# Causal mask of four head pairs: from a product on TensorE to a select on GpSimd, with the staircase loaded as seven rows

## The chip, the cores and the metric

The kernel runs on one core of one Trainium2 chip. The metric is the device time in microseconds (us) from launch to end; lower is better. Engines are called by the profile's short names: PE (TensorE, matmuls), PEld (its weight loads), DVE (VectorE), ACT (ScalarE), POOL (GpSimd) and SP (SyncE, which here only issues DMAs).

## The reference

Two stages. First causal attention with a selective decay, over 8 batches x 8 heads, 576 tokens, head size 64:

```
scores = q @ k.T / 8
cum    = cumsum(max(s, 0))
bias   = min(-(cum[query] - cum[key]), 0)
scores = where(key > query, -1e9, scores + bias)
attn   = softmax(scores) @ v
```

Then a feed-forward block on the 4608 tokens x 512: `h = x @ w_in` (512 to 2048), `g = h * clip(h + 3, 0, 6) / 6`, `out = g @ w_out` (2048 to 512). The output is float32; the kernel multiplies in float16.

## The kernel before

**Pairs and slots.** The 64 heads are taken as 32 pairs, p = 0 to 31; pairs p*4 to p*4+3 belong to one batch (`PPB` = 4). The main loop over p is called a slot here. In slot p PE computes the scores of pair p for both heads (hh = 0, 1), the second head's attention-times-V of pair p-1, the first head's of pair p, and transposes the q and k of pair p+1. From slot 4 on (`p == PPB` has code of its own) matmuls of the feed-forward are strung between these pieces by `group()`: a call takes the next entry of `plan`, "1" for one `m1` (four 128x512 matmuls into a PSUM tile `ph`; then a Relu on ACT into `tr`, L562, and a min-times on DVE into `gT`, L563) or "2" for one `m2` (four into `po`), "." for none. The order on each engine is the program's order; nothing reorders it.

**Scores.** Per head there are three groups, each filling one PSUM bank `S` and followed by one exp on ACT (L422) into the tile `P`. Group 0 has the four diagonal 128x128 blocks (L388), groups 1 and 2 the blocks below the diagonal (L403). The last 64 tokens of both heads are the `corner` (`Sc`, L454; exp into `PC`, L462). From slot 4 on the `S` and `Sc` tiles rotate over two banks, so a group can start only when the exp of the group two before it is done.

**Causal mask of the diagonal blocks, two ways.** For p < `NPROD` = 8 a matmul of 2 x identity with the constant `shut` (minus 65504 above the diagonal) opens the bank: L377, 512 columns, once per head, and L441, 128 columns, once per corner. For p >= 8 this matmul isn't there. Instead rows 68 to 127 of the `qk` tile hold a staircase of 60 steps, so that the scores' own matmul (128 rows instead of 68) pushes most of the masked part far down, and after the exp `shut_out` on POOL (L426, affine_select) sets what lies above the diagonal to zero: `pool_mid` for head 0's group 0, `pool_end` for the corner and head 1's group 0. Their readers are the diagonal blocks of `av(p, hh, 1)` (L481).

**Staircase.** `stair_sb` is loaded once in slot 2; `set_stair` copies it into rows 64 to 127 of a `qk` slot (there are four, pair p uses p % 4): on POOL in slots 5 to 7 (L695, one copy per head), on ACT in slots 8 and 9. Rows 64 to 67 are then overwritten by `load_aug`, two small DMAs that bring the decay's rows.

**Tokens out of order.** Pairs 3 to 6 (`mixed`) have their queries in another order, for which there is a second constant, `shutm`.

**POOL and SP.** In slots 4 to 7 POOL runs, in this order: the loads `tok` of pair p+3 (DMAs issued by POOL), weight chunks (`load_w_in` = `I`, `load_w_out` = `U`), then `pool_mid`: `cast_v(p+1)` (two casts, L206 and L207, which wait for the V of pair p+1) and `set_stair`; then `load_aug`. POOL waits there for no exp. SP issues the loads of V, `load_v(p+2)`, three DMAs each.

Of the kernel before, what the change touches and what calls it, by code (L numbers as in the profile page):

```python
# [10 lines left out]
F16 = mybir.dt.float16  # L11
# [3 lines left out]
NEG_BIG = -1200.0  # L15
# [3 lines left out]
def kernel(  # L19
# [30 lines left out]
    NVRAW = 2  # L50
    VW = 66
    NROW = 1
    NWARM = (11, 2, 6)
    HALVES = (slice(0, 288), slice(288, SEQ))

    grp = (np.arange(128) * 61 // 128)[None, :]
    steps_r = np.arange(1, 61)[:, None]  # L60
    stair = np.zeros((128, 2, 128), np.float32)
    stair[68:, 0] = np.where(grp < steps_r, 1.0, 0.0)
    stair[68:, 1] = np.where(grp == steps_r, NEG_BIG, 0.0)
    stair_dram = nc.inline_tensor(stair.astype(np.float16), name="stair")
# [30 lines left out]
    stair_sb = keep("stair_sb", [128, 2, 128], F16)  # L95
# [63 lines left out]
    def load_aug(p, eng):  # L159
        for hh in range(2):  # L160
            g = 2 * p + hh
            eng.dma_start(  # L162
                out=qks[p % NQK][64:68, hh, :, 64 * hh : 64 * hh + SEQ],
                in_=rows_of[g // 32].rearrange("(r g) i t -> g r i t", g=32)[
                    g % 32, :, slice(0, 3, 2) if mixed(p, 0) else slice(1, 3), 0:SEQ
                ],
            )

    def load_w_in(c):
        nc.gpsimd.dma_start(  # L170
# [102 lines left out]
    def mixed(p, i):  # L273
        return i == 0 and PPB - 1 <= p < NPROD - 1
# [82 lines left out]
    def Pof(p, hh):  # L357
        return Ps[(2 * p + hh) % 3]
# [10 lines left out]
    def scores(p, hh, g):  # L369
        qT, kT = qk_of(p, hh)  # L370
        pt = Pof(p, hh)
        S = s_bank([128, 512], "S")
        by_product = p < NPROD
        if g == 0:
            rows = slice(0, 68 if by_product else 128)
            if by_product:
                mm(  # L377
                    S.rearrange("p (t c) -> p t c", c=128),
                    lhsT=ident2,
                    rhs=(shutm if mixed(p, 0) else shut)[:, None, :].to_broadcast(  # L380
                        [128, 4, 128]
                    ),
                    start=True,
                    stop=False,
                )
            for j in range(4):
                c = slice(128 * j, 128 * (j + 1))
                mm(  # L388
                    S[:, c],
                    lhsT=kT[rows, c],  # L390
                    rhs=qT[rows, c],
                    start=(j == 0 and not by_product),
                    stop=(j == 3 and p >= NROW),
                )
            if p < NROW:
                for j in range(4):
                    c = slice(128 * j, 128 * (j + 1))
                    by_rows(p, hh, S[:, c], c, c, j == 3)
        else:
            for j in ((0, 3) if g == 1 else (1, 2)):  # L400
                c = OFF[j] - 512 * g
                w = 448 - 128 * j
                mm(  # L403
                    S[:, c : c + w],
                    lhsT=kT[0:68, 128 * j : 128 * (j + 1)],
                    rhs=qT[0:68, 128 * (j + 1) : SEQ],
                    start=(c == 0),
                    stop=(c != 0 and p >= NROW),
                )
# [12 lines left out]
        nc.scalar.activation(out=pt[:, c], in_=S, func=AF.Exp, scale=0.125)  # L422

    def shut_out(ap, w):
        part = ap.rearrange("p (t c) -> p t c", c=w)
        nc.gpsimd.affine_select(  # L426
            out=part,
            in_=part,
            pattern=[[0, part.shape[1]], [1, w]],
            compare_op=ALU.is_ge,  # L430
            fill=0.0,
            base=0,
            channel_multiplier=-1,
        )

    def corner(p):
        S = s_bank([128, 2, 64], "Sc")
        by_product = p < NPROD
        rows = slice(0, 68 if by_product else 128)
        if by_product:  # L440
            mm(  # L441
                S,
                lhsT=ident2,
                rhs=(shutm if mixed(p, 0) else shut)[:, None, 0:64].to_broadcast(
                    [128, 2, 64]
                ),
                start=True,
                stop=False,
            )
        for hh in range(2):  # L450
            qT, kT = qk_of(p, hh)
            if p < NROW:
                by_rows(p, hh, S[:, hh, :], slice(512, 640), slice(512, 576))
            mm(  # L454
                S[:, hh, :],
                lhsT=kT[rows, 512:640],
                rhs=qT[rows, 512:576],
                start=(hh == 0 and not by_product),
                stop=(hh == 1),
            )  # L460
# [232 lines left out]
    def set_stair(i, copy, heads=(0, 1)):  # L693
        for hh in heads:
            copy(  # L695
                out=qks[i][64:128, hh, :, 64 * hh : 64 * hh + 640].rearrange(
                    "p i (t c) -> p i t c", c=128
                ),
                in_=stair_sb[64:128, :, None, :].to_broadcast([64, 2, 5, 128]),
            )  # L700

    fill(nc.vector, xT[:, 0, 0:SEQ], 0.0)

    def warm(n):
# [125 lines left out]
    load_aug(1, nc.gpsimd)  # L830
    load_v(1, nc.sync)
    load_aug(2, nc.sync)
    cast_v(0)
    for i in range(2):
        load_qk(3, i)
# [11 lines left out]
    for p in range(NP):  # L847
# [25 lines left out]
                crossbar_qk(p + 2)  # L873

        def pool_mid():
            if p >= NPROD:
                shut_out(Pof(p, 0)[:, 0:512], 128)
            if nxt:
                cast_v(p + 1)
            if p in (5, 6, 7):  # L880
                set_stair((p + 3) % NQK, nc.gpsimd.tensor_copy)
            if p == 13:
                new_rest()
                cum4(1, nc.gpsimd, whole)
                cum5(1, nc.gpsimd.tensor_copy, whole)

        def pool_end():
            if p >= NPROD:
                shut_out(PCs[p % 2][:, 0:128], 64)
                shut_out(Pof(p, 1)[:, 0:512], 128)  # L890
            if p >= NPROD and p != 9 and p + 2 < NP:
                if p == 14:
                    cum6(1, nc.gpsimd, whole)
                load_aug(p + 2, nc.gpsimd)

        if p >= PPB:
            for fn, c in {
                4: ((I, 2),),
                5: ((I, 3),),
                6: ((U, 0), (U, 1), (U, 2), (U, 3)),  # L900
                7: ((U, 4), (U, 5), (U, 6), (U, 7)),
            }.get(p, ()):
                fn(c)
        if PPB <= p < NPROD:
            pool_mid()
            if p == 4:
                load_aug(7, nc.gpsimd)
            elif p in (6, 7):
                load_aug(p + 2, nc.gpsimd)

        if p and p + 2 < NP:
# [40 lines left out]
        if p == PPB:  # L952
            early[0] = False
            scores(p, 0, 0)
            av(p - 1, 1, 0)
            av(p - 1, 1, 1)
            norm(p - 1, 1)
            m1_begin(0, 0, NKC - 1)
            scores(p, 0, 1)
            transpose_x(p - 1)  # L960
            m1_begin(0, 1, NKC - 1)
            pt = transpose_in(p + 1, 0)
            transpose_out(p + 1, 0, pt, pars=(0,))
            group()
            transpose_out(p + 1, 0, pt, pars=(1,))
            scores(p, 0, 2)
            group()
        else:
            scores(p, 0, 0)
            if p >= NPROD:  # L970
                pool_mid()
# [11 lines left out]
        if p == 12:  # L983
            cum2(whole)
        corner(p)
        if p in (8, 9):
            set_stair(3, nc.scalar.copy, (p - 8,))
        elif p == 11:
            new_sum()
            cum1(1, whole)  # L990
        group()
# [3 lines left out]
            get(1)  # L995
            av(p, 0, 0)
        scores(p, 1, 0)
        if p >= NPROD:
            pool_end()
        if PPB < p < NPE - 1:  # L1000
            get(1)
        elif p == 3 * PPB:
# [62 lines left out]
```

## Time and profile before

| | us |
|---|---|
| median of 3 runs (354.74 to 355.49) | 354.82 |
| the profiled execution, whole | 354.79 |
| its span in the profile | 353.1 |
| PE busy in the span | 345.1 (98%) |
| DVE, ACT, POOL busy | 230.2, 224.7, 169.7 |
| L377 matmuls | 16 of 128x512 |
| L441 matmuls | 8 of 128x128 |
| L695 staircase copies | 6 on POOL, 2 on ACT, 1.25 each |

The granted PE clock is full all through. Slots by PE's order in the trace: slot 4 from 25.55 to 34.17, slot 5 to 41.26, slot 6 to 48.39, slot 7 to 57.26, slot 8 to 64.40, slot 9 to 73.64. The profiler's time for one matmul (379 ns for 128x512) overlaps with the next one's; the spacing of starts is what a matmul costs in a row of them.

### The profile page before, as it was taken

What the parts mean: (1) busy time and instruction counts of PE and PEld (TensorE: products, weight loads), DVE (VectorE), ACT (ScalarE), POOL (GpSimd) and SP (SyncE); (2) the same over time, 40 slices, a digit from 0 to 9 for tenths busy, and PEclk for the clock granted to TensorE, in tenths of its full rate; (3) what the DMA queues carried; (4) which work ended last, traced back from release to release, by engine and by line L of the source; (5) the groups of instructions that cost most, each with busy time, mean ns of one, the idle gap of its engine ahead of it and who ended that gap; (6) DMA issues with size and microseconds to landing.
All of it is one profiled execution on the core that took longest, in us unless ns stands there. A gap on an engine that the chain in (4) does not pass through costs nothing.

```text
span 353.1 us, 7778 instructions
## 1 busy us (share of the span) xinstructions
PE 345.1 (98%) x2926; PEld 191.0 (54%) x2926; DVE 230.2 (65%) x476; ACT 224.7 (64%) x397; POOL 169.7 (48%) x296
## 2 busy tenths in 40 slices
PE   8999999999999999999999999999999999999995
PEld 3775666555555555555555555555555444444442
DVE  7996997676868677666666666757654544544531
ACT  6987896787787667666776666666664334443310
POOL 8977799676778656455555555555310000000000
PEclk9999999999999999999999999999999999999999
DMA  9999999999999999998798959997120100101112
GB/s 164 152 208 209 199 185 182 117 181 196 154 136 100 190 219 188 173 211 186 168 167 198 179 144 197 181 180 164 38 75 14 59 29 34 59 2 59 59 50 72
DMA packets 144782, 48.35 MB, mean 137 GB/s; under 512 B 130648, under 2 KB 139784, under 8 KB 144744
## 3 DMA queue, kind: packets, MB, share of 16 engines
q1 hardware_dynamic: 117112, 37.54, 54.0%
q0 software_dynamic: 27392, 10.03, 24.8%
q8 instruction: 23, 0.38, 0.4%
q10 hardware_dynamic: 240, 0.28, 0.2%
q14 instruction: 15, 0.12, 0.1%
HBM read 37.36 MB, written 9.44 MB: 133 GB/s over the span
## 4 chain that ended last, share of the span: by engine, by line
PE 90%; DVE 4%; ACT 3%; issue 1%; DMA 1%; ACTq 0%
PE po L574 35%; PE ph L547 34%; PE O L481 7%; PE S L403 7%; PE S L388 4%; DVE qk L310 1%; PE pt L266 1%; ACT P L422 1%; DMA s_all<-in_s_dram 1%; DVE x L504 1%; PE ptx L518 1%; PE Sc L454 1%; ACT tr L562 1%; PE S L377 1%; DVE qk L332 1%
## 5 line engine op out<-in xcount | busy, mean ns | idle before, releaser
L563 DVE SCALAR_TENSOR_TENSOR gT<-tr,ph 128x512 f16<-128x512 f32 x144 | 98.9, 687 | 97.6 <-ACT tr L562 96.5
L547 PE MATMUL ph<-xT,w_in_sb 128*128 128x512 f16 x576 | 148.1, 379 | 0.0
L574 PE MATMUL po<-w_out_sb,gT 128*128 128x512 f16 x576 | 145.9, 379 | 0.0
L562 ACT ACTIVATE tr<-ph,bias 128x512 f32<-128x512 f32 x144 | 99.0, 688 | 73.0 <-PE ph L547 70.6
L422 ACT ACTIVATE P<-S 128x512 f16<-128x512 f32 x192 | 111.3, 595 | 37.5 <-PE S L388 22.3
L547 PEld LDWEIGHTS <-w_in_sb 128*128 128x128 f16 x576 | 51.4, 97 | 44.2
L574 PEld LDWEIGHTS <-gT 128*128 128x128 f16 x576 | 50.0, 97 | 46.5 <-issue 0.2
L426 POOL TENSOR_SCALAR_AFFINE_SELECT P<-P 128x512 f16<-128x512 f16 x48 | 31.3, 651 | 44.4 <-ACT P L422 44.4
L403 PE MATMUL S<-qk 68*128 68x448 f16 (+3 forms) x256 | 49.0, 272 | 0.5 <-ACT P L422 0.5
L481 PE MATMUL O<-va,P 128*128 128x65 f16 x896 | 47.9, 193 | 0.3 <-ACT P L422 0.3
L481 PEld LDWEIGHTS <-P 128*128 128x128 f16 x896 | 39.2, 97 | 14.0 <-ACT P L422 0.5
L230 DVE COPY qk<-jt 64x768 f16<-64x768 f16 x84 | 36.8, 439 | 1.2
L403 PEld LDWEIGHTS <-qk 68*128 68x128 f16 x256 | 23.7, 98 | 24.5 <-issue 0.9
L162 POOL DMA_DIRECT2D qk<-rows_of x56 | 32.8, 588 | 1.1 <-PE S L403 0.3
L504 DVE TENSOR_TENSOR x<-O,rl 128x320 f16<-128x320 f32 x64 | 31.5, 492 | 2.2
L590 DVE TENSOR_SCALAR ob<-po 128x512 f32<-128x512 f32 (+1 forms) x36 | 24.3, 676 | 8.3 <-PE po L574 7.6
L388 PEld LDWEIGHTS <-qk 128*128 128x128 f16 (+1 forms) x256 | 18.9, 97 | 14.0 <-DVE qk L310 1.7
L426 POOL TENSOR_SCALAR_AFFINE_SELECT PC<-PC 128x128 f16<-128x128 f16 x24 | 7.0, 293 | 39.9 <-ACT PC L462 39.8
L388 PE MATMUL S<-qk 128*128 128x128 f16 (+1 forms) x256 | 24.8, 219 | 1.0 <-DVE qk L332 0.5
L206 POOL CAST va<-vraw 128x512 f16<-128x512 f32 x32 | 21.0, 656 | 4.7 <-DMA vraw<-in_v_dram 2.4
L310 DVE COPY qk<-pt 64x576 f16<-64x576 f16 x22 | 17.6, 805 | 6.2 <-ACT qk L310 5.9
L202 POOL CAST tok<-raw 128x576 f16<-128x576 f32 x28 | 18.0, 679 | 0.0
(79 smaller groups left out, 201.9 us busy)
## 6 DMA issues: line engine op xcount, KB each, us to landing
out_dram<-ob SPq DMA_DIRECT2D x35, 256.0 KB, 2.0
vraw<-in_v_dram SPq DMA_DIRECT2D x64, 128.0 KB, 4.0
raw<-in_q_dram SPq DMA_DIRECT2D x14, 288.0 KB
raw<-in_k_dram SPq DMA_DIRECT2D x14, 288.0 KB
tok<-in_q_dram POOLq DMA_DIRECT2D x18, 144.0 KB, 5.2
tok<-in_k_dram POOLq DMA_DIRECT2D x18, 144.0 KB, 5.9
w_in_sb<-in_moe_w_in_dram POOLq DMA_DIRECT2D x4, 512.0 KB, 8.5
w_out_sb<-in_moe_w_out_dram POOLq DMA_DIRECT2D x8, 256.0 KB, 7.1
```

The lines of the kernel that those rows point to most:

```text
L162: eng.dma_start(out=qks[p % NQK][64:68, hh, :, 64 * hh : 64 * hh + SEQ], in_=rows_of[g // 32].rearrange("(r g) i t -> g r i t", g=32)[g % ...
L230: copies[par](out=qk[0:64, :, i, 128 * par : 128 * par + 256 * n].rearrange("p h (s two c) -> p h s two c", two=2, c=128)[:, :, :, 0, :], ...
L388: mm(S[:, c], lhsT=kT[rows, c], rhs=qT[rows, c], start=(j == 0 and not by_product), stop=(j == 3 and p >= NROW),)
L403: mm(S[:, c : c + w], lhsT=kT[0:68, 128 * j : 128 * (j + 1)], rhs=qT[0:68, 128 * (j + 1) : SEQ], start=(c == 0), stop=(c != 0 and p >= NROW),)
L422: nc.scalar.activation(out=pt[:, c], in_=S, func=AF.Exp, scale=0.125)
L426: nc.gpsimd.affine_select(out=part, in_=part, pattern=[[0, part.shape[1]], [1, w]], compare_op=ALU.is_ge, fill=0.0, base=0, channel_multip ...
L481: mm(o[:, i, :], lhsT=lhsT, rhs=va[:, hh, j, 0:65], **kw)
L504: nc.vector.tensor_tensor(out=X[p][:, :, hh, :], in0=o[:, :, 0:64], in1=rl.to_broadcast([128, 5, 64]), op=ALU.mult,)
L547: mm(ph, lhsT=w_in_sb[:, kc, ft * 128 : (ft + 1) * 128], rhs=xT[:, kc, n * 512 : (n + 1) * 512], start=(kc == 0), stop=(kc == NKC - 1),)
L562: nc.scalar.activation(out=tr, in_=ph, func=AF.Relu, bias=bias3[:, 0:1])
L563: nc.vector.scalar_tensor_tensor(out=gTs[n][:, ft, :], in0=tr, scalar=6.0, in1=ph, op0=ALU.min, op1=ALU.mult)
L574: mm(po, lhsT=gTs[n][:, ft, t4 * 128 : (t4 + 1) * 128], rhs=w_out_sb[:, ft, :], start=(ft == 0), stop=(ft == NFT - 1),)
```

## The change

It does five things.

1. `NMASK` = 4 takes the place of `NPROD` in the choice of mask: pairs 4 to 7 no longer have L377 and L441, and use the staircase and `shut_out`. `shut_out` gets a second index pattern for `mixed` pairs.
2. The staircase has 7 steps of 16 tokens (it had 60). It comes by `load_stair`, a DMA of 7 rows x 6 KB straight into rows 68 to 74 of a `qk` slot, in two versions (`stairm` for mixed pairs). `stair_sb`, its load and all `set_stair` copies are gone. The first one, for pair 4, is issued by SP at the front; pairs 5 to 7 in slot 2; 8, 9, 10 in slots 6, 7, 8.
3. On POOL `pool_mid` and `pool_end` now run from slot 4. The weight chunks stand inside `pool_mid`, after the select and `cast_v`; two of the `U` chunks move from slot 6 to 5, and one from 7 to 6. Three `load_aug` (pairs 7, 8, 9) move from POOL to SP.
4. In slot 4 the third score group of head 0 stands before the second `m1_begin` instead of five pieces later.
5. For the q of pairs 7 to 10 the second half of the copy out of PSUM (`transpose_out`, `pars=(1,)`) comes after the next `group()`.

```diff
+    NMASK = PPB
+    NSTAIR = 7
...
+    def load_stair(p, eng):
+        eng.dma_start(
+            out=qks[p % NQK][68 : 68 + NSTAIR], in_=stair_drams[mixed(p, 0)].ap()
+        )
...
-        by_product = p < NPROD
+        by_product = p < NMASK
         if g == 0:
-            rows = slice(0, 68 if by_product else 128)
+            rows = slice(0, 68 if by_product else 68 + NSTAIR)
...
+    def shut_out(p, ap, w):
         part = ap.rearrange("p (t c) -> p t c", c=w)
+        pattern = [[0, part.shape[1]], [1, w]]
+        if mixed(p, 0):
+            part = part.rearrange("p t (g w v) -> p t g w v", w=4, v=16)
+            pattern = [[0, part.shape[1]], [64, w // 64], [1, 4], [4, 16]]
...
     load_aug(2, nc.sync)
+    load_stair(PPB, nc.sync)
...
         def pool_mid():
-            if p >= NPROD:
-                shut_out(Pof(p, 0)[:, 0:512], 128)
+            shut_out(p, Pof(p, 0)[:, 0:512], 128)
             if nxt:
                 cast_v(p + 1)
-            if p in (5, 6, 7):
-                set_stair((p + 3) % NQK, nc.gpsimd.tensor_copy)
+            for fn, c in {
+                4: ((I, 2),),
+                5: ((I, 3), (U, 0), (U, 1)),
+                6: ((U, 2), (U, 3), (U, 4)),
+                7: ((U, 5), (U, 6), (U, 7)),
+            }.get(p, ()):
+                fn(c)
...
         if p == 2:
-            nc.sync.dma_start(out=stair_sb, in_=stair_dram.ap())
+            for i in range(PPB + 1, NPROD):
+                load_stair(i, nc.sync)
+        if p in (4, 6, 7):
+            n = 7 if p == 4 else p + 2
+            if p != 4:
+                load_stair(n, nc.sync)
+            load_aug(n, nc.sync)
+        elif p == 8:
+            load_stair(10, nc.sync)
...
         if p == PPB:
             scores(p, 0, 0)
+            pool_mid()
...
             scores(p, 0, 1)
             transpose_x(p - 1)
+            scores(p, 0, 2)
             m1_begin(0, 1, NKC - 1)
             pt = transpose_in(p + 1, 0)
             transpose_out(p + 1, 0, pt, pars=(0,))
             group()
             transpose_out(p + 1, 0, pt, pars=(1,))
-            scores(p, 0, 2)
             group()
         else:
             scores(p, 0, 0)
-            if p >= NPROD:
-                pool_mid()
-            get(0)
-            group()
+            pool_mid()
+            if NPROD - 1 <= p + 1 < NPE:
+                pt = transpose_in(p + 1, 0)
+                transpose_out(p + 1, 0, pt, pars=(0,))
+                group()
+                transpose_out(p + 1, 0, pt, pars=(1,))
+            else:
+                get(0)
+                group()
...
         corner(p)
-        if p in (8, 9):
-            set_stair(3, nc.scalar.copy, (p - 8,))
-        elif p == 11:
+        if p == 11:
...
         scores(p, 1, 0)
-        if p >= NPROD:
-            pool_end()
+        pool_end()
```

More of the change, by code (lines that the diff above doesn't have):

```diff
@@ L52 @@
     NROW = 1
+    NMASK = PPB
+    NSTAIR = 7
     NWARM = (11, 2, 6)
     HALVES = (slice(0, 288), slice(288, SEQ))
[L59 to L64, printed above, removed]
+    grp = (np.arange(128) // 16)[None, :]
+    steps_r = np.arange(1, NSTAIR + 1)[:, None]
+    under = np.where(grp < steps_r, 1.0, 0.0)
+    equal = np.where(grp == steps_r, NEG_BIG, 0.0)
+    over = under.reshape(NSTAIR, 2, 16, 4).transpose(0, 1, 3, 2).reshape(NSTAIR, 128)
+    stair_drams = []
+    for name, of_q in (("stair", under), ("stairm", over)):
+        stair = np.zeros((NSTAIR, 2, 2, SPAD), np.float16)
+        for hh in range(2):
+            for i, rows in enumerate((of_q, equal)):
+                stair[:, hh, i, 64 * hh : 64 * hh + 640] = np.tile(rows, (1, 5))
+        stair_drams.append(nc.inline_tensor(stair, name=name))
     cpool = ctx.enter_context(tc.tile_pool(name="consts", bufs=1))
@@ L94 @@
     ident2 = keep("ident2", [128, 128], F16)
-    stair_sb = keep("stair_sb", [128, 2, 128], F16)
     bias3 = keep("bias3", [128, 1], F32)
@@ L422, in scores @@
         nc.scalar.activation(out=pt[:, c], in_=S, func=AF.Exp, scale=0.125)
-    def shut_out(ap, w):
+    def shut_out(p, ap, w):
         part = ap.rearrange("p (t c) -> p t c", c=w)
+        pattern = [[0, part.shape[1]], [1, w]]
+        if mixed(p, 0):
+            part = part.rearrange("p t (g w v) -> p t g w v", w=4, v=16)
+            pattern = [[0, part.shape[1]], [64, w // 64], [1, 4], [4, 16]]
+            if w == 64:
+                part, pattern = part[:, :, 0], [pattern[0]] + pattern[2:]
         nc.gpsimd.affine_select(
@@ L428, in shut_out @@
             in_=part,
-            pattern=[[0, part.shape[1]], [1, w]],
+            pattern=pattern,
             compare_op=ALU.is_ge,
@@ L437, in corner @@
         S = s_bank([128, 2, 64], "Sc")
-        by_product = p < NPROD
-        rows = slice(0, 68 if by_product else 128)
+        by_product = p < NMASK
+        rows = slice(0, 68 if by_product else 68 + NSTAIR)
         if by_product:
@@ L691 @@
     nc.gpsimd.tensor_copy(out=unmix(perm), in_=mix(ident))
[L693 to L700, printed above, removed]
     fill(nc.vector, xT[:, 0, 0:SEQ], 0.0)
@@ L887, in pool_end @@
         def pool_end():
-            if p >= NPROD:
-                shut_out(PCs[p % 2][:, 0:128], 64)
-                shut_out(Pof(p, 1)[:, 0:512], 128)
+            shut_out(p, PCs[p % 2][:, 0:128], 64)
+            shut_out(p, Pof(p, 1)[:, 0:512], 128)
             if p >= NPROD and p != 9 and p + 2 < NP:
@@ L893, in pool_end @@
                     cum6(1, nc.gpsimd, whole)
[L894 to L904, printed above, removed]
-            pool_mid()
-            if p == 4:
-                load_aug(7, nc.gpsimd)
-            elif p in (6, 7):
                 load_aug(p + 2, nc.gpsimd)
@@ L969 @@
             scores(p, 0, 0)
-            if p >= NPROD:
-                pool_mid()
-            get(0)
-            group()
+            pool_mid()
[7 more added lines that the diff above has]
+                group()
             scores(p, 0, 1)
@@ L997 @@
         scores(p, 1, 0)
-        if p >= NPROD:
-            pool_end()
+        pool_end()
         if PPB < p < NPE - 1:
```

## The prediction

> **What bounds the kernel now.** I read the page's busy times first, then the chain that ended last, then the matmuls of slots 4 to 9 in order of time, and last ACT, DVE and POOL in the same stretch.
>
> ```profile
> PE 345.1 (98%) x2926; PEld 191.0 (54%) x2926; DVE 230.2 (65%) x476; ACT 224.7 (64%) x397; POOL 169.7 (48%) x296
> PE 90%; DVE 4%; ACT 3%; issue 1%; DMA 1%; ACTq 0%
> ```
>
> PE is busy 98% of the span and holds 90% of the chain. So the question for each removed matmul is only whether PE stands waiting at that place. The timeline of PE tells it (start, length, line, in brackets a wait):
>
> ```profile
> 25.55 0.38 PE L377 MATMUL S<-shut,ident 128*128 128x512 f16 x1
> 26.13 0.40 PE L388 MATMUL S<-qk 68*128 68x128 f16 x4 [0.20 <-DVE qk L310]
> ...
> 30.71 0.20 PE L481 MATMUL O<-va,P 128*128 128x65 f16 x1 [0.33 <-ACT P L422]
> ...
> 32.78 0.38 PE L403 MATMUL S<-qk 68*128 68x320 f16 x2 [0.33 <-ACT P L422]
> ...
> 37.50 0.22 PE L441 MATMUL Sc<-shut,ident 128*128 128x128 f16 x1
> 37.55 0.22 PE L454 MATMUL Sc<-qk 68*128 68x64 f16 x2
> 37.65 0.38 PE L377 MATMUL S<-shut,ident 128*128 128x512 f16 x1
> 37.86 0.39 PE L388 MATMUL S<-qk 68*128 68x128 f16 x4
> ...
> 71.39 0.38 PE L403 MATMUL S<-qk 68*128 68x320 f16 x2 [0.21 <-ACT P L422]
> ```
>
> Count starts, not lengths: L377 holds PE from 37.65 to 37.86, 0.21 us, and four 512-column matmuls of `m1` take 0.86 us, so 0.216 each; L441 costs 0.055. Slots 5 to 8 have next to no gaps. Slot 4 has four: before 26.13, near 27.87, before 30.71 and before 32.78. Slot 9 has one, before 71.39. ACT shows where that comes from:
>
> ```profile
> 69.46 1.25 ACT L695 COPY qk<-stair_sb 64x1280 f16<-64x1280 f16 x1
> 70.74 0.60 ACT L422 ACTIVATE P<-S 128x512 f16<-128x512 f32 x1
> ```
>
> The exp of head 1's group 0 stands behind a staircase copy; the third group wants its bank. The last thing to see is how full the others are. In one slot (41.26 to 48.39; busy, count):
>
> ```profile
> 41.26:48.39 7.13, 7.13 (x90) 4.71 (x87) 6.74 (x14) 6.44 (x13) 7.02 (x10) 1.00 1.11 169
> ```
>
> PE 7.13, PEld 4.71, DVE 6.74, ACT 6.44, POOL 7.02 of 7.13 us. DVE has 0.4 us to spare.
>
> **What the skill says.** The Trainium skill, "TensorE: Matmul & The Clock Gate", section "Back-to-back issue gap", gives N/2.4 + 2.5 ns at full clock: 216 ns for 512 columns, 56 for 128. The trace agrees (216, 55); the lower sustained figure of the same section, 131 ns for 512, is not seen here. Its section "LDWEIGHTS" says that a load goes by columns, not by contraction rows; here 68-row loads take 98 ns and 128-row ones 97, so 75 rows instead of 68 or 128 cost nothing. "DMA: Bandwidth & Descriptors", section "Issuing engines are not separate DMA queues", says that DMAs of SP and POOL share the same 16 engines. The trace agrees: from 10 to 60 us, while POOL loads weights, a 128 KB V load takes 7.5 us to land (median), over the whole run 4.0 (longest 12.6).
>
> **Part by part.** The sum is made against the profiled execution, 354.79 us (span 353.1 and 1.69 around it), which is the median of the runs, 354.82, to within 0.03.
>
> *Matmuls removed.* 8 of L377 at 0.216 and 4 of L441 at 0.055: 1.73 + 0.22 = 1.95 us of PE time.
> - Slot 4. The first L377 starts at 25.55 and ends by 25.77; the next matmul waits until 26.13 for the k copy of pair 4 (DVE L310, done 26.07). Without L377 PE waits 0.58 instead of 0.36: nothing gained. The rest of the slot is worked with the order of part 4. The third group moves ahead to about 28.15, where its bank has been free since 27.2 (the exp of group 0). Its exp then ends near 29.2 instead of 30.66, and the wait before 30.71 goes (0.50 by starts). The `m1` pieces behind it come 0.2 later (29.27 for 29.07), so the Relu starts at 29.68 for 29.48; but on ACT the exp that stood between the two Relus is gone, so ACT reaches head 1's exp at about 31.86 for 32.14. It ends at 32.45, and that is what the next 32.78 waits for: it becomes about 32.50. PE waits on ACT there as before; it also waits near 30.5 for the bank of the first `m1`, which DVE L563 frees near 31.1. Slot 4 gains **0.28** (bounds 0 and 0.8: nothing moves, or both gaps go).
> - Slots 5, 6, 7. Two L377 and one L441 each, 0.488. The corner's 0.055 I don't count: L377 at 37.65 already waits some 0.03 for its bank (exp of group 2, end 37.59), and this wait grows by what L441 was. So **0.43** each, 1.30 in all; bounds 0.8 (DVE and ACT turn out to be the bound in half of it) and 1.46.
>
> *Split q copies (slots 6 to 9).* The same DVE work in another order, L563 ahead of the second half copy (0.8 us). In slots 6 and 7 an `m1` now waits some 0.057 for its `ph` bank (starts at 45.48 and 52.62, after a row that should end at 45.42 and 52.56). **0.11** gained. Without the split this wait would grow as PE gets faster; that is why I let the gain of slots 5 to 7 stand.
>
> *ACT copies removed (slots 8, 9).* 2 x 1.25 us of ACT. In slot 8 PE waits for nothing at that place: 0. In slot 9 the gap before 71.39 is 0.37 by starts (71.02 to 71.39), and one of 0.10 follows at 73.96, when DVE frees `ph` late because ACT was late. **0.47**; bounds 0.2 and 0.5.
>
> *POOL.* Off: 6 copies x 1.25 = 7.5 us, 6 DMA issues of `load_aug` x 0.59 = 3.5. On: 8 selects of 128x512 x 0.65 and 4 of 128x128 x 0.29 = 6.4 us. The mixed pattern was run once, on `shutm`: 0.34 against 0.29 for the plain one, so 0.65 may be 0.78. All of it lies beside PE, as long as a select is done when its `av` comes. What is new is that POOL waits for exps and that its queue (casts that wait for V, weight DMA issues of 0.71 to 0.80 each) stands ahead of the selects. Played through with the trace's times: slot 4's corner select ends at about 32.5, its reader comes at 33.9; slot 5: 38.9 against 40.5; slot 6: 45.5 against 47.1; slot 7: 52.2 against 54.5. So **0**, with 1.4 us to spare.
>
> *Weights and tokens issued later.* Chunk 2 of `w_in` goes out near 31.9 instead of 28.35. Weight loads took 6.8 to 10.1 us to land, because they queue behind others; it is wanted at 41.0. At the worst figure it lands at 42, 1 us late; but the delay was backlog, and that is smaller by then. The last `w_out` chunk goes out near 51.5 (before: 53.25). Cost 0, bounds 0 and 1.0.
>
> *SP.* On: 7 staircase loads (0.58 us was the one of `stair_sb`) and 6 `load_aug` (0.64 each); off: 1. Two of the extra issues stand ahead of pair 5's V load, which goes out 1.2 us later; the rest fall where SP waits for POOL. 43 KB each, 300 KB against 64 KB, is 1.2 us of the 200 GB/s that slots 2 to 7 move, spread over 40 us. Cost 0 unless V comes too late (below).
>
> Sum: 0.28 + 1.30 + 0.11 + 0.47 = 2.16 us. From slot 10 on PE's starts have no gap over 0.3 us, so the gain should reach the end whole: 354.79 - 2.16 = **352.6 us**.
>
> **Rivals.**
> 1. *ACT and DVE become the bound in slots 5 to 7.* For: PE's slot 6 would shrink to 6.64 and DVE has 6.74 to do; head 1's first scores wait for the bank of group 2. Against: the split moves the urgent DVE work ahead, and ACT has 0.7 to spare. If it happens, the second L377 and L441 of each slot (0.27) are hidden by a longer wait: 0.8 lost, 353.4.
> 2. *POOL's queue stops PE, slower.* Place: the corner block of `av(4, 0, 1)` in slot 4. POOL's second cast waits for pair 5's V, and then come a 0.78 weight issue and the corner's select:
>
> ```profile
> 30.52 0.29 POOL L207 CAST va<-vraw 64x128 f16<-64x128 f32 x1 [0.78 <-DMA vraw<-in_v_dram]
> ```
>
> V landed at 30.5. The select ends 1.4 us after the landing, PE wants it at 33.87, so PE waits if V lands after 32.45, and the whole gain is gone at 34.6, 4.1 us later than now. Three staircase issues ahead of it, where one stood, give 1.2; and as the program lets an SP DMA go only when the eighth before it has landed, its last part now waits for pair 4's V, landed at 26.28. At the longest landing seen, 12.6 us, from 23.7, V comes at 36.3, PE waits 3.85: 354.79 - 2.16 + 3.85 = 356.5. Against: the weight chunk that shared the DMA engines with it (28.35) now comes after it. A landing in between (32.5 to 34) costs up to 1.5.
> 3. *No change that can be measured.* The weights' worst case (1.0) and rival 1 (0.8) together: 354.4.
>
> **How the numbers follow.** A measurement can tell about 0.2%, 0.71 us, from no change: faster is below 354.1. My forecast (352.2 to 352.9): 0.65. Rival 1 or a small wait of rival 2 (352.9 to 353.9): 0.21. Rival 3: 0.07. Rival 2 in full: 0.07. So faster 0.86, same 0.07, slower 0.07. The range 352.1 to 353.9 holds the first two.
>
> **What would show it.** In the profile after: L377 8 times, L441 4 times, L426 56 and 28 times, no L695; PE busy near 343. On PE: slot 4 still with a wait of 0.58 for DVE at its first scores and one before the last group of head 1; slots 5 to 7 shorter by 0.4 to 0.5; no gap in slot 9. POOL's waits on exp start in slot 4. I am wrong if PE's `av` (L481) or a diagonal block waits for POOL, if an `m1` waits for `w_in`, or if a slot from 5 to 7 keeps its length.

## The result, and the profile after

The changed kernel took 354.69 us (median; 354.49 to 355.21) where the kernel before took 354.89 beside it (354.74 to 355.49): ratio 0.9993 [0.9976, 1.0011]. That is no change; the forecast was 352.6 with a range of 352.1 to 353.9. Run again later, 22 times, it had a median of 355.25 against 354.81, ratio 1.0027 [1.0011, 1.0042], with executions from 354.19 to 358.91. So it is at best equal, and it spreads where the kernel before hardly does (354.65 to 356.07 beside it). The profiled executions compared here: 354.79 before, 354.49 after. Their 0.30 lies behind the last instruction: DVE's last one ends at 350.00 and 350.02, and the span ends 3.1 and 2.8 us later. Up to that point nothing is gained.

The page of the changed kernel: busy times, the chain by engine, and the group of the selects.

```profile
PE 344.1 (98%) x2914; PEld 190.8 (54%) x2914; DVE 230.5 (65%) x476; ACT 222.0 (63%) x395; POOL 166.6 (47%) x296
PE 85%; DMA 5%; DVE 5%; ACT 3%; issue 1%; POOL 0%; SPq 0%; ACTq 0%
L444 POOL TENSOR_SCALAR_AFFINE_SELECT P<-P 128x512 f16<-128x512 f16 x56 | 37.8, 674 | 46.9 <-ACT P L434 46.8
```

Twelve matmuls are gone and 56 selects are there, as announced. But PE's busy time fell by only 1.0 us and its share of the chain from 90% to 85%; DVE and DMA took that share. So time went into new waits. To find them, take the same matmul in both timelines and watch the difference of its start:

| same matmul | before | after | shift | change in this stretch | forecast for it |
|---|---|---|---|---|---|
| first `m1` of slot 5 | 34.87 | 35.14 | +0.27 | +0.27 | -0.28 - 0.22 |
| of slot 6 | 41.95 | 41.78 | -0.17 | -0.44 | -0.43 |
| of slot 7 | 49.09 | 48.48 | -0.61 | -0.44 | -0.43 - 0.06 |
| first `m2` of slot 8 | 57.74 | 57.60 | -0.14 | +0.47 | -0.22 - 0.06 |
| the same of slot 9 | 64.88 | 64.75 | -0.13 | +0.01 | 0 |
| `av` early in slot 10 | 75.04 | 74.45 | -0.59 | -0.46 | -0.47 |
| `av` late in slot 10 | 78.82 | 78.53 | -0.29 | +0.30 | 0 |
| `m2` at the end | 345.73 | 345.75 | +0.02 | +0.31 | 0 |

(The second L377 of a slot's sum stands in the tail of the slot before; here each is counted where it stands.) Three stretches gave what was forecast: slots 5, 6 and 9. Four didn't: 4, 7, 10 and the tail; they miss 0.77, 0.75, 0.30 and 0.31 us, together the forecast gain to within 0.05. PE's timeline at these places, start, length, line, in brackets a wait:

```profile
26.13 0.40 PE L400 MATMUL S<-qk 75*128 75x128 f16 x4 [0.41 <-DVE qk L322]
...
29.29 0.60 PE L565 MATMUL ph<-xT,w_in_sb 128*128 128x512 f16 x2
...
33.00 0.38 PE L415 MATMUL S<-qk 68*128 68x320 f16 x2 [0.59 <-ACT P L434]
...
34.08 0.44 PE L499 MATMUL O<-va,P 128*128 128x65 f16 x9
34.56 0.20 PE L499 MATMUL O<-va,PC 128*128 128x65 f16 x1
...
52.23 0.42 PE L278 MATMUL pt<-ident,tok 96*128 96x96 f16 x6 [0.58 <-DVE qk L322]
...
70.89 0.38 PE L415 MATMUL S<-qk 68*128 68x320 f16 x2
```

The first scores start at 26.13 as before, so the first L377 bought nothing, as forecast. The group forecast for 32.50 starts at 33.00, later than the 32.78 before. The corner block is held until 34.56 (its nine neighbours at 34.08 should leave it at 34.36; a gap this short gets no bracket), and the first scores behind it to 34.66. Before 52.23 there is a wait that the kernel before didn't have. Slot 9's wait, before 70.89, is gone.

**Slot 4, the chain on ACT and DVE.** ACT and DVE of the changed kernel, from 30.4 on:

```profile
31.70 0.80 ACT L322 COPY qk<-pt 64x576 f16<-64x576 f16 x1 [0.55 <-DVE qk L310]
32.37 0.58 ACT L434 ACTIVATE P<-S 128x512 f16<-128x512 f32 x1
```

```profile
30.43 0.69 DVE L581 SCALAR_TENSOR_TENSOR gT<-tr,ph 128x512 f16<-128x512 f32 x1 [0.49 <-ACT tr L580]
31.15 0.46 DVE L310 COPY qk<-pt 64x576 f16<-64x576 f16 x1
```

ACT is free early, as I said, since an exp has moved away. But its copy of pair 5's k waits 0.55 us for DVE's second half copy of q; that stands behind `gT`, `gT` behind the Relu, and the Relu behind the `m1` at 29.29, which the third group, moved ahead of it, pushed back from 29.07. So head 1's exp starts at 32.37 for 32.14, and PE's group with it. In the profile before, the same two copies:

```profile
30.93 0.46 DVE L298 COPY qk<-pt 64x576 f16<-64x576 f16 x1
```

```profile
31.47 0.80 ACT L310 COPY qk<-pt 64x576 f16<-64x576 f16 x1
```

There the half copy on DVE ended at 31.39 and ACT's own predecessor at 31.41, so the copy on ACT showed no wait.

**Slot 4, POOL.** POOL of the changed kernel, in the same slot:

```profile
28.84 0.61 POOL L218 CAST va<-vraw 128x512 f16<-128x512 f32 x1 [2.47 <-DMA vraw<-in_v_dram]
...
30.93 0.91 POOL L444 TENSOR_SCALAR_AFFINE_SELECT P<-P 128x512 f16<-128x512 f16 x1
...
32.89 0.29 POOL L219 CAST va<-vraw 64x128 f16<-64x128 f32 x1 [0.49 <-DMA vraw<-in_v_dram]
33.36 0.77 POOL L182 DMA_DIRECT2D w_in_sb<-in_moe_w_in_dram  x1 [0.18 <-issue]
34.14 0.37 POOL L444 TENSOR_SCALAR_AFFINE_SELECT PC<-PC 128x128 f16<-128x128 f16 x1
```

The cast that started at 26.28 before waits 2.47 us for V and starts at 28.84. Pair 5's V lets its cast go at 32.89 (before: 30.52), and behind it come the weight issue and only then the corner's select, 34.14 (the forecast end of 32.5 meant a start near 32.2). This is rival 2's queue. Why is V late? SP issues the first two parts of pair 4's V at the same time in both kernels (from 18.66 before, from 18.73 after), but the last part of pair 5's V, the one that the cast at 32.89 waits for, leaves SP late. SP before, then after:

```profile
22.52 2.37 SPq L154 DMA_DIRECT2D vraw<-in_v_dram  x1
```

```profile
22.28 1.01 SPq L157 DMA_DIRECT2D vraw<-in_v_dram  x2
27.02 0.67 SPq L161 DMA_DIRECT2D vraw<-in_v_dram  x1
```

Three staircase issues stand just ahead of these (21.02 to 22.18), and between the two lines SP waits 3.7 us for an earlier load of V, as rival 2 said it would. The DMA engines differ too. The same stretch in both kernels, first before, then after (length, busy time and count of PE, PEld, DVE, ACT, POOL, then PE clock, DMA share, GB/s):

```profile
24.00:28.00 4.00, 3.78 (x60) 2.59 (x57) 3.63 (x10) 2.85 (x8) 2.50 (x5) 1.00 1.26 216
```

```profile
24.00:28.00 4.00, 3.57 (x59) 2.56 (x55) 3.64 (x10) 2.85 (x8) 1.39 (x2) 1.00 1.41 189
```

With the staircase loads in it the packets take longer (1.41 for 1.26; this share adds up the packets' times, and passes 1 where they overlap) and less is moved (189 GB/s for 216). The profiled executions of the experiments below, fourteen with these two, agree. In all seven with the three loads in slot 2 the share is 1.34 to 1.47, and SP has the last part of pair 5's V out only at 26.7 to 28.6, after 1.5 to 4.3 us of waiting for a load of V. In the seven without them there it is 1.16 to 1.30, and the part is out at 24.7 to 25.3. Pair 4's cast starts at 27.37 to 29.56 with them and at 26.13 to 28.15 without, so these two ranges overlap.

**Slot 7, DVE.** The k transposes of pair 8 at 52.23 use the PSUM bank that its q had. DVE of the changed kernel:

```profile
49.98 0.79 DVE L322 COPY qk<-pt 64x576 f16<-64x576 f16 x1
50.67 0.66 DVE L581 SCALAR_TENSOR_TENSOR gT<-tr,ph 128x512 f16<-128x512 f32 x1
51.37 0.80 DVE L322 COPY qk<-pt 64x576 f16<-64x576 f16 x1
```

The split put `gT` between the half copies; the second ends at 52.17, and PE, which could have begun the transposes at 51.48 (before: 52.31), stands until then.

**Slot 10, DVE against POOL.** From pair 11 on a transposing DMA, the crossbar, brings q and k into the tile `jt`. DVE's two copies of it, SBUF to SBUF, the kernel before first, and POOL beside them in the changed kernel:

```profile
75.17 1.41 DVE L230 COPY qk<-jt 64x768 f16<-64x768 f16 x2
```

```profile
74.67 2.01 DVE L242 COPY qk<-jt 64x768 f16<-64x768 f16 x2
```

```profile
74.70 0.66 POOL L444 TENSOR_SCALAR_AFFINE_SELECT P<-P 128x512 f16<-128x512 f16 x1
75.29 0.64 POOL L218 CAST va<-vraw 128x512 f16<-128x512 f32 x1
```

The pair took 1.41 us before, when POOL's select came 0.4 us after them (75.60), and takes 0.65 further on with no POOL work beside it; here it takes 2.01, `gT` comes behind it, and an `m1` waits for its bank. The Trainium skill, "SBUF — State Buffer", section "SBUF: two separate sides", says that GpSimd and a DVE operation in a two-port mode share a pair of ports as an exclusive lock: whichever starts first has it for its whole instruction. One of the two copies took 1.71 of the 2.01 and ended at 76.38, 0.22 us behind the second cast, which fits a wait for the whole row of select and casts; that this copy runs in such a mode is not shown.

### The profile page after: what moved, and what is told of

Its sections match the earlier page's. It is cut to its first block, busy times and chain, and to the rows that moved or that the text cites. A ratio compares the mean times of both kernels' runs of the same rounds, so it can differ in the third digit from the quotient of the medians.

```text
span 352.8 us, 7771 instructions
## 1 busy us (share of the span) xinstructions
PE 344.1 (98%) x2914; PEld 190.8 (54%) x2914; DVE 230.5 (65%) x476; ACT 222.0 (63%) x395; POOL 166.6 (47%) x296
## 4 chain that ended last, share of the span: by engine, by line
PE 85%; DMA 5%; DVE 5%; ACT 3%; issue 1%; POOL 0%; SPq 0%; ACTq 0%
PE po L592 34%; PE ph L565 32%; PE O L499 7%; PE S L415 6%; PE S L400 3%; DMA vraw<-in_v_dram 3%; DMA tok<-in_k_dram 1%; DVE qk L242 1%; DVE gT L581 1%; DVE qk L322 1%; PE pt L278 1%; ACT P L434 1%; ACT tr L580 1%; DMA s_all<-in_s_dram 1%; DVE x L522 1%
## 5 line engine op out<-in xcount | busy, mean ns | idle before, releaser
L444 POOL TENSOR_SCALAR_AFFINE_SELECT P<-P 128x512 f16<-128x512 f16 x56 | 37.8, 674 | 46.9 <-ACT P L434 46.8
L169 POOL DMA_DIRECT2D qk<-rows_of x50 | 29.8, 598 | 2.2 <-PE S L400 1.6
L444 POOL TENSOR_SCALAR_AFFINE_SELECT PC<-PC 128x128 f16<-128x128 f16 x28 | 8.5, 304 | 43.0 <-ACT PC L480 42.9
L400 PEld LDWEIGHTS <-qk 75*128 75x128 f16 (+1 forms) x256 | 18.8, 97 | 12.9 <-DVE qk L322 1.4
L400 PE MATMUL S<-qk 75*128 75x128 f16 (+1 forms) x256 | 24.8, 219 | 0.9 <-DVE qk L322 0.6
```

Of the source, the lines that this page charges most:

```text
L169: eng.dma_start(out=qks[p % NQK][64:68, hh, :, 64 * hh : 64 * hh + SEQ], in_=rows_of[g // 32].rearrange("(r g) i t -> g r i t", g=32)[g % ...
L400: mm(S[:, c], lhsT=kT[rows, c], rhs=qT[rows, c], start=(j == 0 and not by_product), stop=(j == 3 and p >= NROW),)
L444: nc.gpsimd.affine_select(out=part, in_=part, pattern=pattern, compare_op=ALU.is_ge, fill=0.0, base=0, channel_multiplier=-1,)
```

## The experiments

Edits are against the changed kernel unless said otherwise. Each was timed beside the kernel before (354.74 in the first two groups, 354.81 in the third), so medians of different groups were not measured side by side. In the second group the kernel before was itself disturbed: 10 of its 75 executions took over 355.5, one 359.31.

### One cause at a time, then together

*pair8_whole*: the q copy of pair 8 not split.

```diff
-            if NPROD - 1 <= p + 1 < NPE:
+            if NPROD - 1 <= p + 1 < NPE and p + 1 != NPROD:
```

> The changed kernel, but pair 8's q copy is not split (both halves before the group, as before the change). Theory 1 (named stalls): in slot 7 the k transposes of pair 8 share the one bank 't' with its q, and wait for the late second half of the q copy. The gap of 0.75 us near 51.4 shrinks to 0.15 to 0.25 (the second half now ends at about 51.6, PE wants the bank at 51.5), so 0.5 to 0.6 us less: about 354.1. Theory 2 (absorber): something after slot 9 paces the run, so the gain is visible up to slot 9 and gone by 265 us: 354.5 to 354.7. Rival for the gap alone: it is DVE's total work in slot 7, not the order; then a gap of 0.6 or more stays.

Median 355.25, ratio 1.0024 [1.001, 1.0037]; profiled 354.16. PE and DVE in slot 7:

```profile
51.36 0.42 PE L278 MATMUL pt<-ident,tok 96*128 96x96 f16 x6
...
52.08 1.02 PE L565 MATMUL ph<-xT,w_in_sb 128*128 128x512 f16 x4 [0.30 <-DVE gT L581]
```

```profile
49.69 1.62 DVE L322 COPY qk<-pt 64x576 f16<-64x576 f16 x2
51.34 0.69 DVE L581 SCALAR_TENSOR_TENSOR gT<-tr,ph 128x512 f16<-128x512 f32 x1
```

Counted from the `m1` ahead of them (49.96 here, 50.25 in the changed kernel), the transposes come 0.58 us sooner, but the `m1` behind them now waits for `gT`. By starts the slot loses 0.17 + 0.47 = 0.64 us instead of 0.75, as the rival in the expectation had it. The order of DVE's work moves the wait and hardly shortens it.

*copies_first*: in slot 4 both half copies of q before the next `group()`.

```diff
-            transpose_out(p + 1, 0, pt, pars=(0,))
+            transpose_out(p + 1, 0, pt)
             group()
-            transpose_out(p + 1, 0, pt, pars=(1,))
```

> The changed kernel, but in slot 4 both halves of pair 5's q copy stand before the first group (as everywhere else). Theory 1: in slot 4 the k copy on ACT waits for the second half of the q copy on DVE, this for the first product into gT on DVE, this for the Relu on ACT, this for the first m1. With the halves first, the second half ends near 30.4 instead of 31.6, the k copy starts at about 31.1 instead of 31.7, head 1's exp at about 31.8 instead of 32.37, and the matmul that now starts at 33.00 starts at 32.4. The corner's select on POOL is not earlier (it ends at 34.5), so the wait for it grows by as much, to 0.7 to 0.8: the time stays at 354.6 to 354.7. Rival (the k copy waits for ACT's own queue): the 33.00 stays.

Median 355.56, ratio 1.0016 [1.0005, 1.0027]. ACT and PE:

```profile
31.08 0.80 ACT L322 COPY qk<-pt 64x576 f16<-64x576 f16 x1
31.73 0.59 ACT L434 ACTIVATE P<-S 128x512 f16<-128x512 f32 x1
```

```profile
32.10 0.65 PE L415 MATMUL S<-qk 68*128 68x448 f16 x4
...
35.34 0.20 PE L499 MATMUL O<-va,PC 128*128 128x65 f16 x1 [1.45 <-POOL PC L444]
```

The copy on ACT and the exp start 0.6 us sooner, and head 1's two groups run in one row (x4) with no wait. The chain of the last section is shown. All of it is then lost 1.8 us later at the corner, where PE waits 1.45 for POOL, twice what was expected: PE arrives 0.6 us earlier, and the select starts later too (34.92 for 34.14), behind a cast that starts only at 33.67.

*stair_later*: the staircases of pairs 5 to 7 loaded a slot later (`if p == 2:` becomes `if p == 3:` at `load_stair`).

> The changed kernel, but the staircase loads of pairs 5 to 7 are issued by SP in slot 3, behind pair 5's V, instead of in slot 2 ahead of it. Theory 1: in the changed kernel POOL's load_aug for pair 6 waited for a staircase load into the same qk tile, and V of pair 4 landed 2.5 us later than before; the whole POOL queue of slot 4 was late and PE waited 0.27 at the corner block of slot 4. With the loads later: POOL's casts of pair 4 start near 26.3 instead of 28.84, the corner select ends near 32.5, no wait of PE near 34.4, 0.27 us less: about 354.4. Rival (V is late because SP and the DMA engines carry more, wherever it stands): casts stay after 28, the wait stays.

Median 354.49, ratio 0.9997 [0.9989, 1.0005]. The first cast of slot 4 starts at 26.54, near the 26.28 before, the stretch 24 to 28 is back at a DMA share of 1.25 with 206 GB/s, and slot 4's corner wait is gone. But one slot later the same reader waits:

```profile
42.45 0.20 PE L499 MATMUL O<-va,PC 128*128 128x65 f16 x1 [1.49 <-POOL PC L444]
```

So the loads delay pair 5's V. That they delay the next one when moved isn't shown: here the cast of pair 6's V waits 2.17 us and starts at 38.42, but in *all_mended*, with the loads at the same place, it starts at 35.93 without a wait.

*all_mended*: the three edits together.

> The three mends together. Theory 1: they add, and open what each hides: 0.6 of slot 4's chain, 0.27 of the corner, 0.5 to 0.6 of slot 7: 353.2 to 353.4. Theory 2 (absorber after slot 9): PE is 1.9 us ahead of the kernel before at slot 9 and falls back by 265 us; the time is 354.3 or more.

Median 354.88 (353.24 to 357.76), ratio 0.9996 [0.9982, 1.0011]. The profiled execution, 353.95, has neither slot 4's corner wait nor the one before head 1's last group, and is 1.5 us ahead at slot 7, then loses 0.64 in slot 7, 0.51 in slot 8 to two `m2` that wait for `w_out`, and 0.30 in slot 10. In other executions it is 3 us slower than before. So the expected 353.2 to 353.4 came in the fastest executions, not in the median. What varies was still in it.

### What varies: POOL's order

*selects_first*: in slots 4 to 7 `cast_v` behind the slot's selects.

```diff
-            if nxt:
+            if nxt and p >= NPROD:
                 cast_v(p + 1)
...
+            if p < NPROD:
+                cast_v(p + 1)
```

(the second one at the end of `pool_end`).

> The changed kernel, but in slots 4 to 7 POOL's two casts of the next pair's V stand behind the slot's selects instead of between the first and the others. Nothing else. Theory 3 (queue): runs differ because the landing of V differs, and V's landing reaches PE only through POOL's order: casts wait for V, the corner's select is queued behind them, PE waits for the select. With the casts last, no gap of PE at a corner block in slots 4 and 5, and the spread of the runs (3.3 us for the same kernel with pair 8 unsplit, 2.4 with the copies first) falls to under 1; the median goes to 354.2 to 354.4. Rival (the DMA engines' speed reaches PE by the weights and tokens as well): the corner gap goes, but gaps at po (w_out) or ph stay and the spread stays over 2 us.

Median 354.42 (354.09 to 355.94), ratio 0.9988 [0.9973, 1.0002]. POOL and PE of the profiled execution:

```profile
29.56 0.61 POOL L218 CAST va<-vraw 128x512 f16<-128x512 f32 x1 [3.47 <-DMA vraw<-in_v_dram]
...
33.24 0.39 POOL L444 TENSOR_SCALAR_AFFINE_SELECT PC<-PC 128x128 f16<-128x128 f16 x1
34.37 0.65 POOL L218 CAST va<-vraw 128x512 f16<-128x512 f32 x1
```

```profile
34.37 0.19 PE L499 MATMUL O<-va,PC 128*128 128x65 f16 x1
```

V is later than ever (3.47), yet the corner's block runs without a wait, since the next cast stands behind its select. Slot 5's corner has no wait either. The middle half of the 22 runs lies from 354.2 to 354.96, against 355.03 to 356.56 for the changed kernel as it is (*changed_again*, below, in another group). But the whole spread, 1.85 us, is more than the 1 us expected, and two kernels with POOL's order as it was are about as narrow: *stair_later*, 354.2 to 354.96, and *third_v_buffer*, 354.38 to 355.25. That the wait comes from this queue is shown; how much of the spread does is not.

*third_v_buffer*: `NVRAW = 3` for 2, so that V's load waits for no buffer.

> The changed kernel with three buffers for the raw V instead of two, so that a V load waits for a cast one slot older and goes out earlier; POOL's order is as in the changed kernel. Theory 3: POOL no longer waits for V in slots 4 and 5, the corner gap goes, spread under 1 us, 354.2 to 354.4, as with the selects first. Rival (V is late because the DMA engines are full, whenever it is issued): the casts still wait for V over 1 us in slot 3 or 4, and the time stays at 354.6 or more.

Median 354.95, ratio 0.9997 [0.998, 1.0013].

```profile
29.48 0.61 POOL L218 CAST va<-vraw 128x512 f16<-128x512 f32 x1 [2.99 <-DMA vraw<-in_v_dram]
```

The wait for V stays, with 0.57 at the corner, and SP still waits 4.3 us for an earlier load of V ahead of the last part of pair 5's. V is not late for want of a buffer.

*mended_selects_first*: *all_mended* with *selects_first*.

> All three mends (pair 8 whole, slot 4's copies first, staircases later) and the casts behind the selects. Theory 3: the fast runs of the three mends alone (353.2 to 353.5) become the rule: median 353.2 to 353.5, spread under 1. Rival (weights): gaps at po in slot 8 near 59 and 63 as before (0.25 each) or larger, median 353.8 or more, spread over 2.

Median 353.91, ratio 0.9976 [0.9959, 0.9992]: 0.24% less, the first with an interval below 1. Its median and its spread (353.22 to 356.24) are nevertheless those of the rival, weights, in the expectation. In the profiled execution, 353.39, no `m2` of slot 8 waits, so what spreads the others isn't known.

*act_half*: that, and the first half of pair 8's q copied by ACT: `transpose(p + 1, 0, (nc.scalar.copy, nc.vector.tensor_copy))`.

> The kernel before this one in the list, and the first half of pair 8's q copy on ACT instead of DVE. Theory (slot 7 is bound by DVE's total work: with and without the split PE lost 0.64 to 0.75 there): with 0.8 us of DVE's work gone, the two gaps in slot 7 (0.17 and 0.47) shrink to 0.1 or less together; 0.5 us less than without: 352.7 to 353.0. Rival (order, not load): the gaps stay at 0.6 together.

Median 354.21, ratio 0.9983 [0.9965, 1.0002]; not told apart from the one before it, and far from the 352.7 to 353.0 expected. PE in slot 7:

```profile
50.72 0.42 PE L278 MATMUL pt<-ident,tok 96*128 96x96 f16 x6
50.98 1.03 PE L565 MATMUL ph<-xT,w_in_sb 128*128 128x512 f16 x4
```

Transposes and `m1` follow on each other without a wait: 0.8 us less on DVE takes both its waits away, so in slot 7 DVE was the bound. But a wait of 0.27 before the scores at 50.50, for ACT, and one of 0.29 at 55.90 stand in their place, so little of the 0.64 is kept: behind DVE the next bound is close. The execution itself, 355.78, lost 0.95 at the corner of slot 8, where the cast still stands ahead of the selects, and 1.23 at 69.33 for a DMA of `xT`.

### The parts alone

*changed_again*: the changed kernel as it is.

> The changed kernel once more, for the spread of its runs beside the same runs of the kernel before. Theory 3 (POOL's queue passes the landing of V on to PE): spread over 2 us where the first four runs showed 0.7, the best runs near 354.1 (no wait at the corner), the median 354.6 to 355.2. Rival (the first four runs tell it all): all within 354.4 to 355.3.

355.25, as told above. Its profiled execution took 357.55 and shows the bad case. POOL, then PE, then the stretches:

```profile
33.69 0.61 POOL L218 CAST va<-vraw 128x512 f16<-128x512 f32 x1 [3.33 <-DMA vraw<-in_v_dram]
...
35.66 0.37 POOL L444 TENSOR_SCALAR_AFFINE_SELECT PC<-PC 128x128 f16<-128x128 f16 x1
```

```profile
36.08 0.23 PE L499 MATMUL O<-va,PC 128*128 128x65 f16 x1 [1.57 <-POOL PC L444]
...
37.04 1.91 PE L565 MATMUL ph<-xT,w_in_sb 128*128 128x512 f16 x4
```

```profile
37.00:38.00 1.00, 1.00 (x7) 0.45 (x5) 0.78 (x3) 0.40 (x1) 1.00 (x2) 0.50 0.82 114
38.00:39.00 1.00, 1.00 (x4) 0.35 (x3) 0.20 (x1) 0.01 (x1) 0.99 (x3) 0.50 1.22 202
```

V comes at 33.69, PE waits 1.57 us for the corner's select, and then PE runs at half its clock until about 39.5 us (third number from the end; 0.52 from 36 to 37, 0.77 from 39 to 40): four `m1` matmuls take 1.91 us where 1.03 is the rule. From the corner's block to the first scores of head 1 it is 4.84 us (36.08 to 40.92); in the other execution it was 3.35 (34.56 to 37.91). So the wait costs 1.5 us more than its length, and the two together are the 3.06 us between these two executions, to within 0.1.

*mask_alone*: without the split and with the third score group at its old place.

> The changed kernel without the split of the q copies and with the third score group of slot 4 at its old place: the masks, staircases, POOL's and SP's order alone. Theory 1: in slot 4 the last group of head 1 starts at 32.8 (33.0 in the changed kernel), because the first m1 ends 0.22 us earlier; in slots 6 and 7 the m1 behind the k transposes waits 0.3 to 0.5 for its bank. Best runs 354.1 to 354.4, median 354.4 to 355. Rival (the move helps in slot 4): that group starts at 33.3 or later.

Median 355.83, ratio 1.003 [1.0014, 1.0046], above the 354.4 to 355 expected; the profiled execution, 354.31, is one of the fastest.

```profile
32.65 0.38 PE L415 MATMUL S<-qk 68*128 68x320 f16 x2 [0.55 <-ACT P L434]
```

This execution reached slot 4 0.13 us earlier than that of the kernel before, so 32.65 is the 32.78 of the kernel before: without the move the group isn't late, and without the mask's matmuls it isn't early. The move alone cost the 0.22. Slot 6, not split, has a wait of 0.56 at 44.5, and slot 7 one of 0.47.

*split_alone*: the kernel before with the split q copies only.

> The kernel before with the split of the q copies alone (pairs 7 to 10). Theory 1: PE waits at the k transposes of pair 8 in slot 7 for the bank, 0.2 to 0.3 us by the kernel before's times, and the two waits of 0.057 go: 354.7 to 355.0, spread as before. Rival (the split is a gain of 0.11 as forecast): no gap at those transposes, 354.6.

Median 354.81, ratio 0.9999 [0.999, 1.0007]. The two waits of 0.057 in slots 6 and 7 are gone, and one of 0.17 stands before pair 8's k transposes (52.57 us), for the shared bank: the split gives and takes the same.

*cast_last_10*: *mended_selects_first*, with the cast behind the selects in slot 10 too.

```diff
-            if nxt and p >= NPROD:
+            if nxt and p >= NPROD and p != 10:
...
-            if p < NPROD:
+            if p < NPROD or p == 10:
```

> Three mends and casts behind the selects, in slot 10 too. Theory (DVE's copy of the crossbar's output, SBUF to SBUF, stands while POOL works between SBUF and SBUF: 1.71 us for a copy that takes 0.36 elsewhere, beside a select and a cast back to back): with the cast away only the select is beside it, the copy takes 0.6 to 0.9 and the gap of 0.30 near 76 is under 0.05; median 0.2 to 0.3 below the same kernel without (353.9). Rival (the copy waits for its data from the crossbar): it stays at 1.5 or more and the gap stays.

Median 353.61 (353.25 to 353.83, 5 runs), ratio 0.9962 [0.995, 0.9974]: ahead of both kernels, and the lowest median of all, though *mended_selects_first* was not timed beside it. DVE and PE in slot 10:

```profile
73.63 1.23 DVE L242 COPY qk<-jt 64x768 f16<-64x768 f16 x2
```

```profile
75.89 0.39 PE L400 MATMUL S<-qk 75*128 75x128 f16 x4
76.11 1.03 PE L565 MATMUL ph<-xT,w_in_sb 128*128 128x512 f16 x4
```

With the casts away the two copies take 1.23 instead of 2.01 us, the first ending 0.21 us behind the select, the `m1` follows at once, and slot 10's 0.30 is back. The rival, a wait for the crossbar's data, falls.

## Why the prediction was wrong

**Right: the matmuls' price, and slots 5, 6 and 9.** The counts came out; -0.44 and -0.44 for 0.43 and 0.49, -0.46 for 0.47. That the first L377 would buy nothing held too. In slots 5 and 6 the rival with ACT and DVE as the bound fell, and *mask_alone* shows why: without the split slot 6 waits 0.56.

**Wrong step 1: "So 0, with 1.4 us to spare" for POOL.** In the execution recorded first it costs the least of the four, but in others the most. The spare time was played through with V's landing from the profile before, though the same edits put more loads ahead of V and the same text said that the V loads ranged up to 12.6 us. It cost 0.27 us by starts there, in *changed_again* 1.57 and 1.5 for the clock; *selects_first* takes the wait away. Rival 2 had the mechanism, down to SP's wait for pair 4's V, the place and nearly the point (a wait if V lands after 32.45: it let the cast go at 32.89); in full it was given 0.07, and it lacked the price of the clock. A mixed select took 0.91 us where 0.65 to 0.78 was reckoned, which took another part of the spare time.

**Wrong step 2: slot 4's "gains 0.28".** The sum followed ACT's queue alone ("ACT reaches head 1's exp at about 31.86") and skipped the copy that stands ahead of that exp, which waits for DVE. The term was -0.22 (*mask_alone*, without the move, 0), and with *copies_first* the group runs 0.70 us sooner than in the changed kernel, counted from the `m1` at 31.24 and 31.17.

**Wrong step 3: slot 7.** The largest single part in the execution recorded first: the 0.22 and the split's 0.06 there became a loss of 0.47. This is rival 1, in the one slot where k shares q's bank. DVE's load in the slot before it, in the changed kernel (columns as above):

```profile
41.30:48.00 6.70, 6.70 (x88) 4.47 (x84) 6.51 (x13) 6.13 (x12) 6.69 (x12) 1.00 1.22 200
```

DVE has 0.2 us of 6.70 to spare even where nothing is lost. *pair8_whole* (0.64 lost in the other order) and *act_half* (no wait for DVE) settle that it is DVE's load and not its order, with ACT next behind it.

**Wrong step 4: "the gain should reach the end whole".** PE's gaps were looked at, not what comes near in time on the other engines. In slot 10 an earlier select and cast met DVE's copies: 0.30, given back by *cast_last_10*. From 80 to 265 us another 0.3 goes, in pieces of 0.05 or less. It is no lead being used up: *changed_again*, 2.8 us behind the kernel before at 80 us, loses the same 0.3. With the starts compared one by one over this stretch, 0.19 of it comes at the score groups with the staircase (about half at the corners, half at the groups 0), a few ns a group, in each of eight executions with the 75 rows; in *split_alone*, with 128 rows, it is 0.04. The prediction had put 75 rows at nothing. No run was aimed at it, and why it is so stays open.

**Weights and SP.** No `m1` waited for `w_in`, as said. For `w_out` the bound of 1.0 was not idle: once the front was 1.5 us faster, in *all_mended*, `m2` waited 0.51. Calling SP's added loads 0 was wrong as part of step 1: with them in slot 2 SP holds pair 5's V back, in seven executions of seven. Why V's landing differs so much from one execution to the next was not settled; that it isn't the buffer is shown, and that the DMA engines are busier is only seen.

## What to carry to other kernels

When work moves from the engine that is the bound to one with time to spare, write down what stands ahead of it in that engine's queue, and put each wait there at its longest landing, not at the one the profile happened to show; put work that someone waits for ahead of work that itself waits for a DMA. Before a removed instruction is counted as time, follow the next two waits behind it to the instruction that ends them, on every engine: two releasers that end within 0.1 us of each other look like none. And compare the same instruction's start in both traces, stretch by stretch; the sum hid seven effects of 0.3 to 0.5 us.

## What the runs showed of the hardware

- PE's clock fell to 0.50 for about 3.4 us after a wait of 1.57 us, which cost 1.5 us on top of the wait; two of 0.59 had ended 3.3 and 1.5 us before it began. After waits of 1.45 in *copies_first* and 1.49 in *stair_later* it stayed at 1.00. The Trainium skill, "TensorE: Matmul & The Clock Gate", Part 1, "What's actually happening", has the clock fall after an idle window of about 3.4 us, and says that the window runs freely; here 1.57 in one piece was enough, once in three such waits. Its section "A second HAM failure mode: psum-queue depth-cycling" tells of falls by frequent short idling, which would fit the two waits ahead; that wasn't tried.
- A select of 128x512 with the mixed pattern took 0.91 us; the plain one took 0.66.
- DVE's copy of 64x768 from SBUF to SBUF took 0.36 us with POOL idle, 0.92 with a select on POOL beside it and 1.71 with a select and two casts.
- Score groups with 75 contraction rows instead of 128 started some ns later each, 0.19 us in all over 21 slots; the loads of 68 and 128 rows had shown no difference (98 and 97 ns).
